# Attention and a mixture of experts on one core: order constants refitted, later rows of the second batch, one more unit in blocks

## The chip, the cores and the metric

The kernel runs on one core of a Trainium2 chip. The metric is the device time of one execution in microseconds; the time of a kernel is the median of its runs. TensorE (PE) does the matmuls, with its weight loads shown apart as PEld; VectorE (DVE) and ScalarE (ACT) take results out of the accumulation banks and form sums; GpSimd (POOL) and SyncE (SP) mostly issue DMAs.

## What is computed

Four batches of windowed attention with four sink columns, whose output feeds a mixture of four experts. Every expert works on every token; its result is weighted by a normalised probability.

```python
# q, k, v: 4 batches, 8 heads, 768 rows, 64 columns; n_sink 4, window 128
keep = is_sink | in_window                 # columns 0..3, and the last 128 up to the row
scores = where(keep, q @ k.T / sqrt(64), -1e9)
a = exp(scores - max(scores)); a = a / (sum(a) + 1e-9)
x = (a @ v) laid out as 3072 tokens x 512
# x: 3072 x 512; w1: 4 x 512 x 1024; w2: 4 x 1024 x 512
p = domain_probs / (sum(domain_probs) + 1e-9)
for e in range(4):
    out += p[:, e:e+1] * (relu(x @ w1[e]) @ w2[e])
```

All matmuls take bf16 operands.

## The kernel before

**Tiles and stages.** Each batch `b` has three groups `g` of 256 tokens, and each group four head pairs. Attention on a group has a score step for each pair (L679, into banks named `sps`), exponentials on ScalarE (L704), a mask on VectorE (L698, or L713 in batch 0), the value step (L738 and L745, banks `od`), reciprocals (L772) and a scaling (L784 on ScalarE). The normalised rows are turned into `xT`, by TensorE in batch 0 (L803) and by a DMA from SP after that (L762).

**Rows of q and k.** They come by POOL's DMA queue in tiles of 128 rows (`load_nat`, L229, into `qkn`). In batch 0 TensorE turns them (L573). From batch 1 on, `turn_nat` (L241) turns a tile with a transposing DMA from SP into `qkT`. There is one `qkT` buffer, so a batch's tiles can be turned only after the last scores of the batch before it. The first scores of a batch need its first two tiles, group 1 two more, and from batch 2 on one set of sink scores (L640) needs all six. V comes by `load_v` (L294) into six tiles `vx`, each free after the values of the batch before.

**The experts.** A unit is one (batch, group, expert). A plain unit does `x @ w1` in 32 matmuls of 256 columns (L1053, banks `hps`). A unit in blocks ("fast", `emit_fast`) does the same as a 2 x 2 block product in Winograd's form: seven products P1 to P7 of 8 matmuls of 128 columns (L1140, banks `cps`), with sums between them on VectorE (L1193, L1208) and copies on ScalarE (L1186, L1199). It needs sums of the weights (`weight_form1`, L372 to L378, four for an expert, the last in place of a quarter of w1) and of the tokens (L1109). `START` says from which (batch, group) on an expert's units are in blocks. The second layer is plain in batch 0 (L1392, 512 columns) and in the block form in the others (L1314, 256 columns), with sums of w2 from `weight_form` (L336 to L342) and of the activations (L1237, L1258).

**The order.** The program is written out instruction by instruction by a planner in the kernel itself. It keeps a clock for each engine (`t["pe"]` and so on), and in each turn picks the next piece for TensorE: a step of attention, a part of a unit, a product of the second layer. Each comes with the time at which the planner thinks it is ready and a rank; the lowest rank among the ready ones wins. Work of VectorE and ScalarE is put into a list with a ready time and a slack (`later`), and `flush` emits, in order of due time, what fits. All engines run their instructions in the order that comes out, and wait for one another by semaphores; so the planner's constants set the order and nothing else. `turned_at` is the planner's time for a turned tile, `next_form` queues the next weight sum on VectorE (w1 first), and `ahead` is the batch whose attention is being interleaved (0 during the first).

```python
if ahead:
    next_form()
if ahead + 1 < B and not att.more() and ... mix.done >= sum(work[:ahead]) * LEAD[ahead - 1]):
    ahead += 1
    att = Attention(ahead)
...
opts = [(max(r, now), (DUE if due else 3) - 0.1 * (step == "two"), "att", step) for r, step in att.options()]
```

Of the kernel before, what the change touches and what calls it, by code (L numbers as in the profile page):

```python
# [16 lines left out]
def kernel(  # L17
# [17 lines left out]
    E, Dm, F = moe_w1.shape  # L35
# [22 lines left out]
    ]  # L58

    NGATE = 5  # L60
    START = {0: (1, 0), 1: (0, 2), 2: (0, 0), 3: (2, 1)}
    MIX = 3
    SHARE_OF = (0.98, 0.90, 1.01)
    LEAD = (0.91, 0.90)
    DUE = 1.5
    LOW_PRODUCT = 2.005
    LOW_SECOND = 2.7
    HIGH_PRODUCT = 1.9
    EARLY = 0.01
    MASK = 2500  # L70
    GATE = 1500
    GATE0 = 500
    FORM = 9000
    TOKEN = 1000
    MARGIN = 2000
    HOLD = 0
    FULL = 7
    STEP0 = 0.3
    READY = 40
    WIDE = 2  # L80
    OPEN = 2.6
    ONACT = 1
    ONE = 2
    PAIR = 1
# [3 lines left out]
    BIASED = 1  # L88
    FAST = tuple(START)
    BZ = 0  # L90
# [9 lines left out]
    FLIP, LATE, SLOW = 300, 2500, 1500  # L100
# [78 lines left out]
    landed = {}  # L179
# [12 lines left out]
    def sp(*deps, issue=530, takes=600, turning=False):  # L192
        t["sp"] = max([t["sp"], *deps]) + issue
        at = max(t["hw"], t["sp"] + 800)
        row = next((x[3] for x in moved if x[1] <= at < x[2]), 0.0)
        if turning and row:
            t["hw"] = at + TURNED * (row + SHARE)
            t["sw"] += TURNED * SHARE
            for x in moved:
                if x[2] > at:  # L200
                    x[1] += TURNED * SHARE * (x[1] > at)
                    x[2] += TURNED * SHARE
                    landed[x[0]] = x[2] + 900
                    if x[0][0] == "w1" and ("w1", x[0][1]) in landed:
                        landed["w1", x[0][1]] = max(landed["w1", x[0][1]], x[2] + 900)
        else:
            t["hw"] = at + takes + max(0.0, min(takes, t["sw"] - at)) * (not turning)
        return t["hw"] + 900
# [15 lines left out]
    qkn_free, scored_at = [0.0] * NQB, {}  # L224
# [12 lines left out]
    def turn_nat(b, tb):  # L237

        if b not in qkT:
            qkT[b] = sb.tile([P, 2, NHP, S], BF16, name="qkT", tag="qkT", bufs=1)  # L240
        nc.sync.dma_start(  # L241
            out=qkT[b][:, :, :, tb * P:(tb + 1) * P].rearrange("c i h p -> c (i h) p"),
            in_=nat[b, tb].rearrange("p i h d -> p (i h d)"), transpose=True,
        )
        turned_at[b, tb] = sp(landed["qk", b, tb], scored_at.get(b - 1, 0.0), issue=1330, takes=1400, turning=True) + LATE
        qkn_free.remove(1e12)
        qkn_free.append(turned_at[b, tb])
        qkn_free.sort()
# [106 lines left out]
    spared_at = {}  # L355
    forms1, formed1, forms1_at, left1 = {}, {}, {}, [NG * START[e][0] + START[e][1] for e in range(E)]

# [33 lines left out]
    def form_due(e):  # L391
        n = formed.get(e, 0)
        if e == E - 1 and spared_at.get("w2", 1e12) > t["pe"]:
            return False
        return landed.get(("w2", e), 1e12) + 9000 < t["pe"] and (n < 3 or n == 3 and e in used)
# [3 lines left out]
    def next_form():  # L399

        if forming:
            return False
        x = next(((weight_form1, e) for e in FAST if form1_due(e)), None) or next(
            ((weight_form, e) for e in range(E) if form_due(e)), None)
        if x is None:
            return False

        def run(engine):
            forming.clear()
            x[0](x[1])  # L410
        forming.append(x)
        later("dve", t["pe"], FORM, run)
        return True
# [143 lines left out]
    turned_at, sinkA_at, aT_at, onat_at, xT_at = {}, {}, {}, {}, {}  # L557
# [362 lines left out]
    class Mixture:  # L920
# [25 lines left out]
        def is_fast(self, b, g, e):  # L946
            return (b, g) >= START[e]

# [49 lines left out]
        def firsts(self):  # L998
# [12 lines left out]
            if n < WIDE and early:  # L1011
                at, g = self.next_early()
                yield at, (OPEN if n else 2), ("early", g)
            if n < WIDE and self.units and early <= MIX and self.room() and not (early + zero and self.live >= NH - 1):
                yield self.unit_ready(*self.units[0], False), (OPEN if n else 2) - EARLY, ("unit",)

# [68 lines left out]
        def tokens(self):  # L1085
# [22 lines left out]
            def run(engine):  # L1108
# [4 lines left out]
                else:  # L1113
                    self.T_at[b, g] = done
            later("dve", at, TOKEN, run)

        def emit_fast(self, u, m, ready):
# [64 lines left out]
            if m == "P1":  # L1182
                u["last"] = join(2, lambda at: gated(H[:, 1, :, 1], tiles["X"], 1, at, GATE, slots["X"]))

# [19 lines left out]
            elif m == "P2":  # L1204
                gated(H[:, 0, :, 1], y, 1, end, GATE, slots["Y"])
            elif m == "P7":
# [5 lines left out]
            elif m == "P3":  # L1212
                gated(H[:, 0, :, 0], y, 0, end, GATE, slots["V"])
            else:
# [212 lines left out]
    ahead, upto, loaded, wide = 0, 0.0, 0, 0  # L1427
# [22 lines left out]
    while mix.more() or att.more():  # L1450
        now = t["pe"]

        if not att.more() and ahead == B - 1 and not wide:
            wide = 1
            mix.widened()
        if not att.more() and not loaded:
            loaded = 1
            gates_by_row()
            turns += [(1, tb) for tb in range(NQB)]
            loads.append((load_w1, 3))  # L1460
            for tb in range(NQB):
                loads.append((load_nat, 1, tb))
                if tb % 2:
                    loads += [(load_v, 1, (tb - 1,)), (load_v, 1, (tb,))]
            loads.append((load_w2, 3))
        x = next((x for x in loads if load_ready(x) < now + 1500), None)
        if x and t["pool"] < now + 1500 and free_ring(x):
            loads.remove(x)
            x[0](*x[1:])
        if turns and (ahead < 2 or not mix.second) and landed.get(("qk", *turns[0]), 1e12) < now and (turns[0][0] <= ahead or turns[0][0] == ahead + 1 and not att.todo):  # L1470
            x = turns.pop(0)
            turn_nat(*x)
            b = x[0]
            if b in (1, B - 1) and x[1] == NQB - 1:
                spare_rows("w2" if b == 1 else "w1")
            if 0 < b < B - 1 and x[1] == NQB - 1:
                nc.gpsimd.tensor_copy(out=held, in_=qkT[b][:, 1, NHP - 1, S - 2:S])
                pool(2, turned_at[x])
                nat_loads(b + 1, range(NQB))
                turns += [(b + 1, tb) for tb in range(NQB)]  # L1480
        flush(now)
        mix.tokens()
        mix.chore()
        if ahead:
            next_form()
        if ahead + 1 < B and not att.more() and (ahead == 0 or (ahead + 1, 0) in turned_at) and (ahead == 0 or mix.done >= sum(work[:ahead]) * LEAD[ahead - 1]):
            ahead += 1
            att = Attention(ahead)
            upto = mix.done
        share = (sum(work[:ahead]) - upto) * SHARE_OF[max(ahead - 1, 0)]  # L1490
        due = ahead == 0 or att.steps * share <= (mix.done - upto) * att.total
        opts = []
        if att.more():
            opts = [(max(r, now), (DUE if due else 3) - 0.1 * (step == "two"), "att", step) for r, step in att.options()]
        s2, p = mix.second_ready(), mix.product_ready()
        behind = max(t["dve"] - now, 0.0) + 500 * sum(x[2] == "dve" and x[0] < now + 300 for x in pend)
        opts.append((max(p, now), HIGH_PRODUCT if behind > BEHIND or mix.live >= FULL else LOW_PRODUCT, "product", None))
        opts += [(max(f, now), p, "first", x) for f, p, x in mix.firsts()]
        opts.append((max(s2, now), 1 if mix.since >= 1 else LOW_SECOND, "second", None))
        soonest = min(o[0] for o in opts)  # L1500
        if soonest > now + 40 and flush(soonest, True):
            continue
        if soonest < 20000 and soonest > now + 220:
            idle_products(acc[1], 1, G)
            continue
        if soonest > 1e11:
            if loads:
                x = loads.pop(0)
                x[0](*x[1:])
            else:  # L1510
                turn_nat(*turns.pop(0))
            continue
        r, _, kind, step = min(opts, key=lambda o: (o[0] > now + 40, o[0] if o[0] > now + 40 else 0, o[1]))
        assert r < 1e11
        if kind == "att":
            att.emit(step)
        elif kind == "first":
            mix.emit_first(step, r)
        elif kind == "product":
            mix.emit_product()  # L1520
        else:
            mix.emit_second()
# [36 lines left out]
```

## Time and profile before

| | |
|---|---|
| median of 3 runs | 364.03 us (363.68 to 364.74) |
| the profiled execution | 364.39 us |
| its span, first to last instruction | 362.7 us |
| granted TensorE clock | 1.000 |
| matmuls, weight loads | 4400, 4412 (rows in the trace) |
| idle time of ScalarE before L1186 | 44.0 us, for TensorE |
| idle time of POOL before L1477 | 31.5 us, for turning copies |

The profile is of one execution. A group line gives the source line, the engine, the operation, output and inputs, and how many there were; "idle" is the time in which the engine stood still just before, with what ended it. An engine's idle time matters only if TensorE in the end waits for it. In the timeline the first two columns are the start and the length in us, and a bracket gives the wait just before. The shown length of a matmul is longer than the distance to the next one, since matmuls overlap; distances between starts tell the rate.

```profile
q0 software_dynamic: 77520, 17.31, 55.0%
q1 hardware_dynamic: 38668, 18.75, 25.5%
```

These are the two large DMA queues, with packets, MB and the share of the time of 16 DMA engines: q0 is POOL's (loads), q1 holds SP's.

### The profile page before, as it was taken

What the parts mean: (1) busy time and instruction counts of PE and PEld (TensorE: products, weight loads), DVE (VectorE), ACT (ScalarE), POOL (GpSimd) and SP (SyncE); (2) the same over time, 40 slices, a digit from 0 to 9 for tenths busy, and PEclk for the clock granted to TensorE, in tenths of its full rate; (3) what the DMA queues carried; (4) which work ended last, traced back from release to release, by engine and by line L of the source; (5) the groups of instructions that cost most, each with busy time, mean ns of one, the idle gap of its engine ahead of it and who ended that gap; (6) DMA issues with size and microseconds to landing.
All of it is one profiled execution on the core that took longest, in us unless ns stands there. A gap on an engine that the chain in (4) does not pass through costs nothing.

```text
span 362.7 us, 10537 instructions
## 1 busy us (share of the span) xinstructions
PE 354.3 (98%) x4400; PEld 298.7 (82%) x4412; DVE 298.7 (82%) x669; ACT 164.1 (45%) x417; POOL 71.5 (20%) x92
## 2 busy tenths in 40 slices
PE   8899999899999999999999999999999999999996
PEld 4585767666768878899899899999999999999985
DVE  6854998976598979869989979979999799897850
ACT  5864733569554683842554455455213222313210
POOL 8935116500816151150200000000000000000000
DMA  9999999999999989499871211322012012100011
GB/s 167 166 184 195 210 212 158 127 169 206 150 171 136 151 118 149 55 186 146 124 95 33 58 60 34 42 74 62 17 38 74 24 44 60 31 31 31 2 61 58
DMA packets 117291, 37.25 MB, mean 103 GB/s; under 512 B 100612, under 2 KB 112740, under 8 KB 117244
## 3 DMA queue, kind: packets, MB, share of 16 engines
q0 software_dynamic: 77520, 17.31, 55.0%
q1 hardware_dynamic: 38668, 18.75, 25.5%
q8 instruction: 34, 0.56, 0.6%
q10 hardware_dynamic: 1056, 0.52, 0.5%
q14 instruction: 13, 0.11, 0.1%
HBM read 40.45 MB, written 6.34 MB: 129 GB/s over the span
## 4 chain that ended last, share of the span: by engine, by line
PE 78%; DMA 16%; POOL 2%; DVE 1%; ACT 1%; issue 1%; SPq 0%
PE acc L1314 31%; PE cps L1140 29%; PE hps L1053 7%; DMA w<-in_moe_w_dram 7%; DMA qkn<-in_k_dram 6%; PE acc L1392 5%; DMA qkT<-qkn 3%; PE sps L679 2%; PE od L745 2%; POOL qkn L229 1%; PE od L738 1%; POOL vx L294 1%; ACT aT L704 1%; POOL sel L482 0%; PE sinks L640 0%
## 5 line engine op out<-in xcount | busy, mean ns | idle before, releaser
L1140 PEld LDWEIGHTS <-w 128*128 128x128 bf16 x1152 | 71.8, 98 | 4.4 <-issue 1.5
L1314 PEld LDWEIGHTS <-H 128*128 128x128 bf16 x600 | 55.8, 98 | 6.1 <-issue 0.6
L704 ACT ACTIVATE aT<-sps 128x512 bf16<-128x512 f32 (+1 forms) x96 | 47.1, 577 | 16.2 <-PE sps L679 16.0
L1173 DVE SCALAR_TENSOR_TENSOR H<-cps,gates 128x512 bf16<-128x512 f32 x78 | 52.8, 683 | 0.8
L1140 PEld LDWEIGHTS <-vf 128*128 128x128 bf16 x744 | 45.9, 98 | 2.3 <-issue 0.8
L1314 PE MATMUL acc<-w,H 128*128 128x256 bf16 x360 | 47.7, 273 | 0.0
L1053 PE MATMUL hps<-xT,w 128*128 128x256 bf16 x384 | 47.3, 273 | 0.0
L1392 PE MATMUL acc<-w,H 128*128 128x512 bf16 x180 | 43.6, 379 | 0.9 <-issue 0.5
L1140 PE MATMUL cps<-T,w 128*128 128x128 bf16 x576 | 43.9, 219 | 0.5 <-DVE cps L1193 0.5
L784 ACT ACTIVATE onat<-od,R 128x64 bf16<-128x64 f32 x144 | 33.4, 331 | 24.0 <-DVE R L772 23.9
L1140 PE MATMUL cps<-xT,w 128*128 128x128 bf16 x576 | 43.4, 219 | 0.0
L1186 ACT COPY cps<-cps 128x512 f32<-128x512 f32 x36 | 20.7, 575 | 47.8 <-PE cps L1140 44.0
L1053 PEld LDWEIGHTS <-w 128*128 128x128 bf16 x384 | 36.1, 98 | 5.9 <-issue 0.8
L1140 PE MATMUL cps<-T,vf 128*128 128x128 bf16 x496 | 37.5, 219 | 0.0
L1392 PEld LDWEIGHTS <-H 128*128 128x128 bf16 x192 | 18.0, 98 | 18.1 <-issue 0.3
L294 POOL DMA_DIRECT2D vx<-in_v_dram x24 | 21.6, 913 | 42.0 <-PE od L745 30.1
L1314 PEld LDWEIGHTS <-S 128*128 128x128 bf16 x288 | 27.0, 98 | 3.1 <-issue 0.4
L1193 DVE TENSOR_TENSOR cps<-H,cps 128x512 f32<-128x512 f32 x30 | 20.7, 691 | 9.3 <-PE cps L1140 9.3
L698 DVE TENSOR_TENSOR aT<-aT,mask 128x1024 bf16<-128x1024 bf16 (+1 forms) x36 | 22.8, 639 | 5.7 <-ACT aT L704 5.7
L1364 ACT COPY osb<-acc 128x256 f32<-128x256 f32 x28 | 10.5, 383 | 35.6 <-PE acc L1314 35.6
L1208 DVE TENSOR_TENSOR H<-H,cps 128x512 f32<-128x512 f32 x30 | 20.5, 682 | 4.2 <-PE cps L1140 4.0
L1066 ACT ACTIVATE H<-hps 128x512 bf16<-128x512 f32 x27 | 16.1, 597 | 16.2 <-PE hps L1053 15.8
(128 smaller groups left out, 561.0 us busy)
## 6 DMA issues: line engine op xcount, KB each, us to landing
w<-in_moe_w_dram POOLq DMA_DIRECT2D x7, 1024.0 KB, 16.7
out_dram<-osb SPq DMA_DIRECT2D x19, 256.0 KB
gates<-gate_rows SPq DMA_DIRECT2D x36, 128.0 KB
vx<-in_v_dram POOLq DMA_DIRECT2D x24, 128.0 KB, 6.9
qkn<-in_q_dram POOLq DMA_DIRECT2D x22, 128.0 KB, 6.7
qkn<-in_k_dram POOLq DMA_DIRECT2D x22, 128.0 KB, 6.8
w<-in_moe_w_dram POOLq DMA_DIRECT2D x2, 512.0 KB, 8.8
out_dram<-aT SPq DMA_DIRECT2D x4, 256.0 KB
```

Of the source, the lines that this page charges most:

```text
L294: nc.gpsimd.dma_start(out=vx[tb][:, :, 0:D], in_=v[b, :, tb * P:(tb + 1) * P, :].rearrange("h p d -> p h d"),)
L698: nc.vector.tensor_mul(a, a, m[:, None, :].to_broadcast([P, 2, w]))
L704: nc.scalar.activation(out=a[:, ph], in_=sps[ph][:, 0:w], func=AF.Exp, scale=scale)
L784: nc.scalar.mul(o[:, qi, hp, ph * D:(ph + 1) * D], od[:, qi, ph, 0:D], R[:, qi, ph])
L1053: nc.tensor.matmul(h[:, i].rearrange("p (q n) -> p q n", q=2), lhsT=w1_sb[e][:, db, fb * P:(fb + 1) * P], rhs=xT[b, g][:, :, db], start=(i ...
L1140: nc.tensor.matmul(y[:, f], lhsT=A[:, d, f * P:(f + 1) * P], rhs=T[:, d], start=(m in ("P1", "P5") and f == 0 and d == 0), stop=(d == 1), ...
L1173: nc.vector.scalar_tensor_tensor(out=dst, in0=src, scalar=0.0, in1=gate, op0=ALU.max, op1=ALU.mult)
L1186: nc.scalar.copy(out=tiles["Y"], in_=y)
L1193: nc.vector.tensor_add(tiles["V"], c5, tiles["X"])
L1208: nc.vector.tensor_add(c5, c5, y)
L1314: nc.tensor.matmul(x, lhsT=self.operand(b, g, e, m)[:, f], rhs=forms[e][m][:, f], start=(k == 0 and f == 0 and m in (("P1", "P5", "P2") if ...
L1392: nc.tensor.matmul(op, lhsT=H[:, fb // QF, fb % QF, s], rhs=w2_sb[e][:, fb, :], start=(fb == 0), stop=(fb == NFB - 1),)
```

## The change

Only constants of the planner change, and three conditions:

- `START[0]` goes from (1, 0) to (0, 2): the unit of batch 0, group 2, expert 0 is done in blocks.
- The planner counts a turned tile of batch 1 as ready 1500 ns later (`ROWS1`); the copy itself is the same.
- `next_form` may be called from planner time 21000 ns on (`SOON`), also while the first batch's attention runs; in that time it takes sums of w1 only, since sums of w2 now need `ahead`.
- The ranks and slacks of the planner: attention that is due has rank 0 instead of 1.5 (`DUE`), a product has rank 1 instead of 1.9 when VectorE is behind (`HIGH_PRODUCT`), units of batch 1 may start while four units of batch 0 are left instead of three (`MIX`), attention of batches 2 and 3 starts later (`LEAD`), and the due times of gated evictions (`GATE`), token sums (`TOKEN`) and second-layer sums (`MARGIN`) move.

```diff
-    START = {0: (1, 0), 1: (0, 2), 2: (0, 0), 3: (2, 1)}
-    MIX = 3
+    START = {0: (0, 2), 1: (0, 2), 2: (0, 0), 3: (2, 1)}
+    MIX = 4
     SHARE_OF = (0.98, 0.90, 1.01)
-    LEAD = (0.91, 0.90)
-    DUE = 1.5
+    LEAD = (0.92, 0.94)
+    DUE = 0
...
-    HIGH_PRODUCT = 1.9
+    HIGH_PRODUCT = 1
...
-    GATE = 1500
+    GATE = 3000
...
-    TOKEN = 1000
-    MARGIN = 2000
+    TOKEN = 5000
+    MARGIN = 1000
...
+    SOON = 21000
+    ROWS1 = 1500
...
-        turned_at[b, tb] = sp(landed["qk", b, tb], ..., turning=True) + LATE
+        turned_at[b, tb] = sp(landed["qk", b, tb], ..., turning=True) + LATE + ROWS1 * (b == 1)
...
-            ((weight_form, e) for e in range(E) if form_due(e)), None)
+            ((weight_form, e) for e in range(E) if ahead and form_due(e)), None)
...
-        if ahead:
+        if ahead or now > SOON:
             next_form()
```

The two lines added among the constants move every later line number up by two; the text keeps the numbers of the kernel before.

More of the change, by code (lines that the diff above doesn't have):

```diff
@@ L244, in turn_nat @@
         )
-        turned_at[b, tb] = sp(landed["qk", b, tb], scored_at.get(b - 1, 0.0), issue=1330, takes=1400, turning=True) + LATE
+        turned_at[b, tb] = sp(landed["qk", b, tb], scored_at.get(b - 1, 0.0), issue=1330, takes=1400, turning=True) + LATE + ROWS1 * (b == 1)
         qkn_free.remove(1e12)
```

## The prediction

> **What bounds the kernel now.** I read the page's busy shares first, then its chain and its slices.
>
> ```profile
> PE 354.3 (98%) x4400; PEld 298.7 (82%) x4412; DVE 298.7 (82%) x669; ACT 164.1 (45%) x417; POOL 71.5 (20%) x92
> ...
> DVE  6854998976598979869989979979999799897850
> ...
> PE 78%; DMA 16%; POOL 2%; DVE 1%; ACT 1%; issue 1%; SPq 0%
> ```
>
> TensorE is busy almost throughout, and the chain runs through it for 78% of the span. The 16% of DMA all lies before 72 us, where TensorE has other work while rows and weights land. Busy does not mean dense, so next I asked for the merged chain in order of time, where long pieces give the price of one matmul.
>
> ```profile
> 137.53 3.49 PE hps L1053 x32
> ...
> 160.60 2.68 PE cps L1140 x48
> ```
>
> A 256-column matmul costs 3.49 / 32 = 109 ns and a 128-column one 2.68 / 48 = 56 ns. From 40 us on, nearly all starts of neighbouring matmuls keep these distances, so the end moves only with the matmul work, with the price of changing to scores and back, and with the few real waits. For those I read the waits of TensorE and the timeline around them.
>
> ```profile
> PE sps L679 <- DMA qkT<-qkn: 0.9, 1, 0.9
> PE cps L1140 <- DVE cps L1193: 0.5, 1, 0.5
> ```
>
> ```profile
> 70.37 0.61 PE L1140 MATMUL cps<-T,w 128*128 128x128 bf16 x8
> 71.89 0.34 PE L679 MATMUL sps<-qkT 64*128 64x256 bf16 x4 [0.91 <-DMA qkT<-qkn]
> 72.16 0.62 PE L1140 MATMUL cps<-T,vf 128*128 128x128 bf16 x8
> 72.62 1.89 PE L1392 MATMUL acc<-w,H 128*128 128x512 bf16 x7
> 74.35 0.35 PE L745 MATMUL od<-vx,aT 128*128 128x65 bf16 x6
> 74.63 0.34 PE L679 MATMUL sps<-qkT 64*128 64x256 bf16 x4
> 74.90 0.28 PE L1140 MATMUL cps<-T,vf 128*128 128x128 bf16 x2
> ```
>
> The first scores of the second batch could have begun at 70.8 (8 matmuls of 56 ns after 70.37, and the change) and begin at 71.89: the turned rows are 1.07 us late by start times. The same rows price a change. Six value matmuls of 29 ns end at 74.52 and the scores start at 74.63; four score rows run two at a time, 384 columns in 0.16, and the next line starts 0.27 after them. So each run of scores costs 0.11 + 0.11, about 0.2 us, beyond its columns. Two other waits are worth naming.
>
> ```profile
> 83.85 0.87 PE L679 MATMUL sps<-qkT 64*128 64x128 bf16 x12
> 84.81 0.22 PE L738 MATMUL od<-vsd,sinkA 128*128 128x130 bf16 x1
> ...
> 102.69 0.62 PE L679 MATMUL sps<-qkT 64*128 64x128 bf16 x12
> 103.24 1.05 PE L1053 MATMUL hps<-xT,w 128*128 128x256 bf16 x8
> ...
> 123.29 0.87 ACT L704 ACTIVATE aT<-sps 128x384 bf16<-128x384 f32 x2 [0.57 <-PE sps L679]
> 123.78 0.61 PE L1140 MATMUL cps<-T,w 128*128 128x128 bf16 x8 [0.53 <-DVE cps L1193]
> ```
>
> Twelve score rows take 0.55 to the next line at 102.69 but 0.96 at 83.85: 0.41 lost there, in waits for the exponentials that free score banks. At 123.04 the last score row is followed by L1140 only 0.74 later instead of 0.14: 0.60 lost to a VectorE sum. Before 40 us there are further gaps, but TensorE's order is the same in both kernels up to about 42 us.
>
> **The change, part by part.** The counts are of the instructions in the two built programs.
>
> *One more unit in blocks (batch 0, group 2, expert 0).* It removes 32 matmuls of L1053 (32 x 109 = 3.49 us) and adds 7 products of 8 matmuls of L1140 (56 x 56 = 3.12): -0.37. Its token sums exist already, for expert 1. VectorE gets three instructions more and ScalarE two, of about 0.6 us each; they lie beside TensorE, and any one without cover costs its 0.6. The weight loads go from 32 to 56, 98 ns each, and stay hidden: the 48 matmuls above have one each and run at 56 ns.
> The Trainium skill (Perfetto Trace Analysis, Identifying the Most-Contended Engine) holds the busy share of weight loads, not that of matmuls, for the measure of how close TensorE is to its limit. Counted so, the 24 loads more would cost 2.35 us and this part would come out at about +2; the 56 ns row does not agree.
>
> *Order refitted.* Scores now stand in 32 unbroken runs instead of 34: 2 x 0.2 = -0.4. The last products, from the last unit to the last store, are the same in number and order: 0.
>
> *Rows counted as ready later.* Ahead of the first score row of the second batch now stand 80 more matmuls of L1140 and 32 fewer of L1053: 4.48 - 3.49 = +0.99 us of TensorE work. The q and k loads and the turning copies stand in the same order on POOL and SP up to there, and their issue is held by earlier landings, so they land as before. TensorE arrives at 70.77 + 0.99 = 71.76 against 71.8: at most 0.1 of the 1.07 stays, -0.97. Bounds: -1.07 if the rows come a little earlier, 0 if they come 1 us later.
>
> *Sums of w1 queued in the first batch.* The four sums for expert 0 (L372 to L378, 0.60 us each back to back) move from about 45 to 57 us to about 25 to 30 us, where the slices show VectorE at 4 to 5 tenths instead of 8 to 9. The w1 of expert 0 landed at 21.4, expert 1 at 36.5 (its first sum now comes near 41): no wait on DMA. Cost 0; uncovered, each delays one handoff by 0.6.
>
> *Handoffs in the new order.* I took every wait of TensorE on VectorE or ScalarE, and compared TensorE's rows between producer and consumer with the rows along the other engine's queue. In the old order this finds shortages of 0.39 and 0.56 us where the trace lost 0.41 and 0.60. In the new order these two are gone. The worst new one is at the first values of batch 2: 0.2 from the scores to ScalarE, 0.87 for two exponentials, 0.56 for the mask make 1.65 with the hop, against 1.5 us of TensorE work (8 matmuls of L1053, one run of 8 score rows, two changes), and an eviction of L1066 may stand ahead: 0.4 short. Five more places are short by 0.03 to 0.11, 0.36 in all. So 1.01 becomes 0.77: -0.24. Bounds: -1.0 (all covered) and +0.6 (one more 0.6 us row in the way).
>
> *SP and POOL.* Batch 2's turning copies now stand behind four output stores instead of two, the last of which gets its data 0.3 us after the scores that free the rows' buffer; with an issue of up to 1.4 that delays them under 2 us, and from those scores to the first that need the rows lie 14.7 us of TensorE work, where 4.6 are needed. On POOL, three value loads of batch 2 pass ahead of the last six q/k loads, 3 x 0.88 = 2.6 us. Those scores of batch 1 end near 110.7 instead of 103.2, so the last of the six lands near 121.8 + 7.5 + 2.6 = 131.9 and is turned 3.6 later, at 135.5; it is needed near 138.4, 5.4 later than before: 0, with 3 us to spare. Batch 3's copies are tighter, and are a rival below.
>
> Sum: -0.37 - 0.4 - 0.97 - 0.24 = -1.98. The span of 362.70 becomes 360.7; 1.69 us lie around it (364.39 - 362.70), so the profiled execution would take 362.4. That execution was 0.36 above the median of the runs, 364.03. From the median the sum gives 362.05. Part of the 0.36 may be the late rows themselves, so I take 362.2, between the two.
>
> **The rivals.**
> *The rows are late again.* For: in the trace fifteen of the sixteen parts of the second tile had counted by 69.90 and the last only at 71.75, a straggler that can fall elsewhere, and 0.1 us is no margin. Against: even the fifteen parts were early by 1.9. If it lands 1 us later, the wait is back: 362.2 + 1.0 = 363.2.
> The Trainium skill (DMA: Bandwidth & Descriptors, Why a DMA increments its semaphore by 16 and not by 1) says that the sixteen engines finish independently and only the full count means landed; the trace agrees, by the two times above.
>
> *Batch 3's rows take over, and the kernel is slower.* Its rows can only be turned after batch 2's last scores. Between those and batch 3's first scores stood 27.3 us of TensorE work; now 8.8 (44 matmuls of L1314, 24 of L1053, 8 of L1140, values and changes). Two turning copies need, from the first issue to the second's landing, 7.2 us at this place in the trace (151.6 to 158.8), 4.6 for batch 2 (103.4 to 108.0), but 13.2 for batch 1 (58.6 to 71.8), among weight loads. At 13.2, with 0.2 to issue, the wait is 4.6: 366.8. It makes the kernel slower from about 10.6 us on. Against: the q/k loads that fill the DMA engines there in the trace wait, in the new order, for these very copies to land, and one value load alone comes between.
>
> *VectorE becomes the bound.* For: 9 tenths in most slices. Against: a 512-element row occupies it 0.60, not the 0.68 shown, as back-to-back starts tell. Four w1 sums in the wrong place: 4 x 0.6 = 2.4, 364.6.
>
> *Weight loads bound.* 24 x 98 ns instead of the 0.37 saved: 362.2 + 0.37 + 2.35 = 364.9.
>
> **How the numbers follow.** The forecast gets 0.68 (own range 361.4 to 363.2: all handoffs covered, or one row more), late rows 0.17, batch 3's rows 0.09, VectorE 0.04, weight loads 0.02. About 0.3%, 1.1 us, is what a measurement of this kernel can tell from no change, so faster means under 362.94. Forecast, with a little of it lost above that line, and a third of the late rows make 0.71 faster; batch 3's rows and a little of VectorE make 0.10 slower; 0.19 remain. The range, 361.2 to 364.2, takes in the forecast and the late rows, and leaves out the last three and some ends.
>
> **What would show it.** Right: the first score row of batch 2 (the second one) starts near 71.8 without a wait over 0.2; 32 runs of scores; L1140 has 56 rows more and L1053 32 fewer at the same 56 and 109 ns; the first values of batch 2 wait about 0.4; the last matmul lies some 2 us earlier. Wrong: a wait on turned rows over 0.5 us at any batch, or new VectorE waits of more than 0.8 in sum.

## The result, and the profile after

| | before | after |
|---|---|---|
| first pair: median (lowest to highest of 6 runs) | 364.15 us (363.34 to 365.11) | 362.32 us (362.24 to 362.44) |
| the profiled execution, and its span | 364.39, 362.7 | 362.36, 360.7 |
| the same pair again, in a later group of runs: median (middle half of the runs) | 364.49 (364.04 to 364.94) | 362.44 (362.02 to 362.84) |

The ratio is 0.9933, with a 95% interval of 0.991 to 0.9957; in the repeat it is 0.9941 (0.9924 to 0.9959). The ratios leave out runs more than 1.5% above the fastest of the same kernel, which takes out six runs, all of them of kernels with a moved DMA. Line numbers after are higher by two: L1142 is the old L1140, L1055 the old L1053, L681 the old L679.

The page of the changed kernel, its busy shares, its VectorE slices and the engines of its chain:

```profile
PE 354.0 (98%) x4436; PEld 297.8 (83%) x4436; DVE 299.2 (83%) x671; ACT 165.6 (46%) x419; POOL 71.3 (20%) x92
...
DVE  6775989896588989789879989969999898897850
...
PE 88%; DVE 6%; ACT 2%; DMA 1%; issue 1%; POOL 1%; ACTq 0%; DVEq 0%
```

The shares of busy time say nothing: TensorE stands at 98% in both. (Twelve matmuls of L1392 have no record in the trace of the kernel before, so the real rise in matmuls is 24 and not 36.) The chain tells the change. Its DMA part falls from 16% to 1%, because the chain no longer runs back through the turned rows at 72 us into the loads; it now stays on TensorE. The slices for 18 to 36 us (the third and fourth digits) rise from 5 and 4 to 7 and 5: those are the sums of w1, moved there.

The groups by line and shape (busy time, mean ns of one, idle time before them), first of the kernel before and then of the changed one, and the pieces of the merged chain after, first for the 256-column and then for the 128-column matmul:

```profile
L1140 PE MATMUL cps<-T,w 128*128 128x128 bf16 x576 | 43.9, 219 | 0.5 <-DVE cps L1193 0.5
L1140 PE MATMUL cps<-xT,w 128*128 128x128 bf16 x576 | 43.4, 219 | 0.0
L1053 PE MATMUL hps<-xT,w 128*128 128x256 bf16 x384 | 47.3, 273 | 0.0
L1140 PE MATMUL cps<-T,vf 128*128 128x128 bf16 x496 | 37.5, 219 | 0.0
```

```profile
L1142 PE MATMUL cps<-T,w 128*128 128x128 bf16 x592 | 45.0, 219 | 0.1
L1142 PE MATMUL cps<-xT,w 128*128 128x128 bf16 x592 | 44.7, 219 | 0.0
L1055 PE MATMUL hps<-xT,w 128*128 128x256 bf16 x352 | 43.6, 273 | 0.0
L1142 PE MATMUL cps<-T,vf 128*128 128x128 bf16 x512 | 37.4, 219 | 0.0
```

```profile
41.70 1.75 PE hps L1055 x16
...
115.77 2.69 PE cps L1142 x48
```

32 plain matmuls are gone and 16 + 16 + 16 more in blocks are seen here (8 others are in a smaller group). The rates are the old ones, 1.75 / 16 = 109 ns and 2.69 / 48 = 56 ns. Next TensorE's waits, as what it waited for, the sum in us, how often and the longest; and its timeline where the old kernel waited for turned rows:

```profile
PE acc L554 <- DVE lent L465: 1.4, 1, 1.4
PE sps L681 <- DVE xT L267: 0.4, 1, 0.4
PE tx L805 <- DVE onat L777: 0.3, 2, 0.2
PE od L747 <- DMA vx<-in_v_dram: 0.3, 1, 0.3
PE od L747 <- DVE aT L700: 0.3, 1, 0.3
```

```profile
70.97 0.61 PE L1142 MATMUL cps<-T,vf 128*128 128x128 bf16 x8
71.42 0.61 PE L1142 MATMUL cps<-xT,w 128*128 128x128 bf16 x8
71.97 0.34 PE L681 MATMUL sps<-qkT 64*128 64x256 bf16 x4
72.24 1.90 PE L1394 MATMUL acc<-w,H 128*128 128x512 bf16 x8
```

The scores of batch 1 start at 71.97, which is 8 matmuls of 56 ns and one change behind 71.42: no wait. In this execution the sixteen parts of the second tile had all landed by 71.25. The wait on DVE aT is the handoff that the prediction put at the first values of batch 2:

```profile
125.17 0.87 ACT L706 ACTIVATE aT<-sps 128x384 bf16<-128x384 f32 x2
125.92 0.51 PE L681 MATMUL sps<-qkT 64*128 64x256 bf16 x8
126.07 0.56 DVE L700 TENSOR_TENSOR aT<-aT,mask 128x768 bf16<-128x768 bf16 x1
...
126.69 0.35 PE L747 MATMUL od<-vx,aT 128*128 128x65 bf16 x6 [0.26 <-DVE aT L700]
```

The exponentials end at 126.04, the mask at 126.63, the values start at 126.69; eight score rows after 125.92 would have let them start 0.33 earlier.

**Where the time came from.** I compared the starts of TensorE's rows from 41 us to the last matmul: 317.96 us before, 315.85 after, 2.11 less. A run of scores that nothing disturbs costs 0.20 us beyond its columns in both traces. The wait for the rows accounts for 0.98 of the 2.11. Two old handoffs (0.41 at 83.85 and 0.59 at 123.04) are gone and two new ones (0.33 at 126.22, 0.11 at 124.69) have come: 0.56. Behind 41 us there are 22 runs of scores instead of 24: 0.41. The unit: 0.37. That is 2.32; 0.2 went back. In part it went to the two runs of 18 score rows behind sink scores, at 82.26 and 98.86: with the sinks each costs 0.57 beyond its score columns, where the old run of 6 behind sinks, at 97.23, costs 0.44.

### The profile page after: what moved, and what is told of

It is laid out like the page before. It is cut to its first block, busy times and chain, and to the rows that moved or that the text cites. A ratio compares the mean times of both kernels' runs of the same rounds, so it can differ in the third digit from the quotient of the medians.

```text
span 360.7 us, 10596 instructions
## 1 busy us (share of the span) xinstructions
PE 354.0 (98%) x4436; PEld 297.8 (83%) x4436; DVE 299.2 (83%) x671; ACT 165.6 (46%) x419; POOL 71.3 (20%) x92
## 4 chain that ended last, share of the span: by engine, by line
PE 88%; DVE 6%; ACT 2%; DMA 1%; issue 1%; POOL 1%; ACTq 0%; DVEq 0%
PE cps L1142 31%; PE acc L1316 29%; PE acc L1394 11%; PE hps L1055 10%; PE od L747 3%; PE sps L681 3%; DVE H L1175 2%; DMA vx<-in_v_dram 1%; ACT aT L706 1%; PE od L740 1%; DVE S L1260 1%; PE tx L805 1%; DVE onat L777 1%; DVE H L1210 1%; DVE osb L1404 0%
## 5 line engine op out<-in xcount | busy, mean ns | idle before, releaser
L1142 PEld LDWEIGHTS <-w 128*128 128x128 bf16 x1184 | 73.6, 98 | 4.2 <-issue 1.3
L1142 PEld LDWEIGHTS <-vf 128*128 128x128 bf16 x768 | 47.0, 98 | 1.9 <-issue 0.3
L1394 PE MATMUL acc<-w,H 128*128 128x512 bf16 x192 | 45.3, 379 | 0.0
L1142 PE MATMUL cps<-T,w 128*128 128x128 bf16 x592 | 45.0, 219 | 0.1
L1142 PE MATMUL cps<-xT,w 128*128 128x128 bf16 x592 | 44.7, 219 | 0.0
L1055 PE MATMUL hps<-xT,w 128*128 128x256 bf16 x352 | 43.6, 273 | 0.0
L1142 PE MATMUL cps<-T,vf 128*128 128x128 bf16 x512 | 37.4, 219 | 0.0
L1055 PEld LDWEIGHTS <-w 128*128 128x128 bf16 x352 | 33.0, 98 | 4.5 <-issue 0.6
L1316 PE MATMUL acc<-wf,H 128*128 128x256 bf16 x176 | 23.8, 273 | 0.0
```

What stands on the lines that cost most here:

```text
L1055: nc.tensor.matmul(h[:, i].rearrange("p (q n) -> p q n", q=2), lhsT=w1_sb[e][:, db, fb * P:(fb + 1) * P], rhs=xT[b, g][:, :, db], start=(i ...
L1142: nc.tensor.matmul(y[:, f], lhsT=A[:, d, f * P:(f + 1) * P], rhs=T[:, d], start=(m in ("P1", "P5") and f == 0 and d == 0), stop=(d == 1), ...
L1316: nc.tensor.matmul(x, lhsT=self.operand(b, g, e, m)[:, f], rhs=forms[e][m][:, f], start=(k == 0 and f == 0 and m in (("P1", "P5", "P2") if ...
L1394: nc.tensor.matmul(op, lhsT=H[:, fb // QF, fb % QF, s], rhs=w2_sb[e][:, fb, :], start=(fb == 0), stop=(fb == NFB - 1),)
```

## The experiments

Each group of runs has its own runs of the kernel before beside it: 364.61 median beside the two padded kernels and the two runs that take a part out of the change, 364.49 beside the repeat and the three parts alone, 364.55 beside the three with a moved DMA, 364.33 beside the last. "Middle half" is the range from the first to the third quartile.

**Is the old time, and its spread, a wait for a landing?** Idle matmuls in front of the first scores of batch 1 tell: where TensorE waits there, they cost nothing.

```diff
         c = 0
+        if b == 1 and b not in scored_at:
+            for i in range(19):
+                nc.tensor.matmul(sps[0][:, 0:P], lhsT=ident, rhs=ident, start=True, stop=True)
```

In the kernel before:

> The kernel before with 19 idle matmuls of 128 columns (19 x 56 ns = 1.06 us of TensorE work, results overwritten) right ahead of the first scores of batch 1, nothing else moved. Theory (the first scores wait for a landing that varies from run to run; without a wait the old order takes 364.39 - 1.07 = 363.32): the padding takes the place of the wait, so the median rises only from about 364.15 to between 364.4 and 364.7, the fastest run lies near 364.4 instead of 363.3, the spread of the runs shrinks from 1.8 us to under 0.9, and the profile shows a wait of under 0.3 us on turned rows. Rival (the wait on the landing is not what the old time and its spread consist of): the padding is paid in full, median 365.2, spread as before.

In the changed kernel:

> The changed kernel with the same 19 idle matmuls at the same place. Theory (TensorE arrives at 71.97 after rows that landed at 71.25, so nothing there waits for a landing): paid in full, 362.32 + 1.06 = 363.4, spread still about 0.2 us. Rival (in the changed kernel the landing still sets the first scores, and the trace only happened to show no wait): less than 0.6 us is added.

The padded old kernel took 364.46 (364.00 to 365.10, middle half 364.17 to 364.78) against 364.61 (363.41 to 367.74, middle half 364.05 to 365.14); ratio 0.999 (0.9975 to 1.0004). The padded new kernel took 363.34 (middle half 363.30 to 363.44). The timeline of the padded old kernel:

```profile
70.59 1.22 PE L677 MATMUL sps<-ident 128*128 128x128 bf16 x19
71.75 0.34 PE L682 MATMUL sps<-qkT 64*128 64x256 bf16 x4
```

In the old kernel 1.06 us of added work costs nothing that can be measured and the scores still start at 71.75, without a wait: the padding stands where the wait stood. In the new one the same work is paid in full, 363.34 - 362.32 = 1.02. The spread shrank in the old kernel as expected, though to 1.1 us and not under 0.9. Not all of the old spread is this wait: the two slowest runs of the kernel before in this group, 367.05 and 367.74, had a mean granted clock of 0.995, and no trace of such a run was kept. Without the wait the two kernels thus take about 364.46 - 1.06 = 363.40 and 363.34 - 1.06 = 362.28; a little waiting may be left in the first, since in three of the eleven traces compared below the rows land later than 71.75. The 2.05 between the kernels in the repeat are 1.12 of TensorE's order and some 0.9 of waiting.

**Is nothing left of that wait?** The changed kernel once more:

> The changed kernel once more, on the chip and beside the kernel before of this group, for a like-for-like pair. Theory (no wait on a landing is left on TensorE's path): 362.3, with the middle half of the runs within 0.2 us, where the kernel before has 1.1. Rival (the small spread of the first six runs was luck, landings still reach the path): a middle half as wide as that of the kernel before.

362.44 median, 361.94 to 363.41, middle half 0.8 us wide. The rival is right: landings still reach the path. Whether the narrow spread of the first six runs was luck or belonged to their chip is not shown; none of the six is as fast as the five fastest here (361.94 to 362.05). The timeline of this profiled execution (362.85):

```profile
71.53 0.61 PE L1142 MATMUL cps<-xT,w 128*128 128x128 bf16 x8
72.44 0.34 PE L681 MATMUL sps<-qkT 64*128 64x256 bf16 x4 [0.30 <-DMA qkT<-qkn]
```

The second tile's last part landed at 72.39 here, 0.57 behind the fifteenth, and TensorE, there at 72.08, waited. Over the eleven traces in which POOL issues its loads in the old order the last part comes between 69.64 and 72.39. TensorE arrives at 70.9 before the change, ahead of most of these, and at 72.0 after it, behind most. The chain of this execution holds 17% of DMA again: a wait of 0.30 us is enough to lead it back through the rows, so that share tells where the chain runs and not how much was lost.

**The parts of the change, one at a time.** The early sums taken out of the changed kernel (`SOON = 1e12`):

> The changed kernel with the sums of w1 queued only from the second batch on, as before (SOON beyond the end). The planner then makes 34 runs of scores instead of 32, with all matmuls the same in number. Theory (a run of scores costs 0.2 us; a handoff short by the distance of the rows costs just that): +0.2 for the runs... in sum 0.19 of TensorE work, and handoffs short by 0.64 (ahead of a plain unit before batch 1's scores) and 0.41 instead of 0.11, 0.11 and 0.41: +0.4. Together 362.32 + 0.6 = 362.9. Rival (the early sums are worth nothing, my costing at 0 taken alone): 362.3 to 362.5. Rival (VectorE is near its bound, and 2.4 us of sums come back): 364.7.

The later rows taken out of it (`ROWS1 = 0`):

> The changed kernel with the turned rows of batch 1 counted as ready at their own time again (ROWS1 0). The planner's order then brings the first scores of batch 1 1.33 us of TensorE work earlier, has 33 runs of scores, and 0.67 us more TensorE work and changes in all. Theory: TensorE arrives at 71.97 - 1.33 = 70.64 while rows land at 71.2 to 71.8, so a wait of 0.6 to 1.2 us is back, and so is a spread of the runs of over 0.8 us; handoffs short by 0.97 near batch 2's first scores and 0.4 near 141 us add about 1.5: 362.32 + 0.67 + 0.9 + 1.5 = 365.4. Rival (the constant only shifts rows, and the handoffs are hidden): 362.3 + 0.9 = 363.2.

363.13 and 365.41, where 362.9 and 365.4 were forecast from counts of rows. Without the early sums the two waits that the count named are there:

```profile
72.38 0.34 PE L681 MATMUL sps<-qkT 64*128 64x256 bf16 x4 [0.26 <-DMA qkT<-qkn]
...
78.47 0.62 PE L1142 MATMUL cps<-T,w 128*128 128x128 bf16 x8
79.61 1.03 PE L1055 MATMUL hps<-xT,w 128*128 128x256 bf16 x8 [0.52 <-ACT onat L786]
```

The first is the landing again (72.34 in that trace); the second is the scaling whose place on ScalarE depends on VectorE's row order: 8 matmuls of 56 ns after 78.47 it could have begun at 78.92, so 0.69 is lost by start times, where 0.64 was counted. Without the later rows the wait on the rows is back, and the handoffs near batch 2's first scores lose 1.2 by start times, where 0.97 was counted (the waits of that kernel):

```profile
PE sps L681 <- DMA qkT<-qkn: 1.0, 1, 1.0
PE tx L805 <- DVE onat L777: 0.5, 3, 0.2
PE cps L1142 <- DVE cps L1195: 0.5, 1, 0.5
PE sps L681 <- DVE xT L267: 0.4, 1, 0.4
PE od L747 <- DVE H L1175: 0.4, 1, 0.4
PE od L740 <- ACT onat L786: 0.4, 1, 0.4
```

One part alone in the kernel before: the unit (`START[0]` to (0, 2)), the later rows (`ROWS1`), the ranks and slacks.

> The kernel before with the unit (batch 0, group 2, expert 0) in blocks and nothing else changed. Theory (TensorE's work falls by 0.22 in the order that the old ranks then give; the first scores of batch 1 come 0.37 earlier in that work, so the wait on the rows grows by as much; handoffs are short by 0.73 near 115 to 120 us, 0.32 near 74, 0.21 and 0.12, against 0.39 and 0.56 before): +0.4 to +0.6 on the kernel before. Rival (the unit is worth its 0.37 by itself): -0.4.

> The kernel before with the turned rows of batch 1 counted as ready 1500 ns later and nothing else changed. The planner then puts 2.62 us more of TensorE work ahead of batch 1's first scores, and makes 36 runs of scores instead of 34. Theory (no wait on the rows: -0.9; 0.57 us more of TensorE work and changes; handoffs short by up to 1.11 near 128 us and 0.49 near 144 instead of 0.95: +0.65): +0.3 on the kernel before, with a middle half of the runs under 0.4 us. Rival (taking that wait away is worth its size in any order): -1.0.

> The kernel before with the refitted ranks, slacks and start points alone (MIX, LEAD, DUE, HIGH_PRODUCT, GATE, TOKEN, MARGIN as in the changed kernel; old START, no later rows, no early sums). Theory (0.42 us more of TensorE work, 35 runs of scores; the first scores of batch 1 at the same work as before, so the same wait and the same spread; handoffs short by 0.39, 0.97 and 1.02 instead of 0.39 and 0.56: +1.4): +1.8 on the kernel before, 366.2. Rival (the refit of the order is a gain by itself, 0.64 by my sum): -0.6.

| alone in the kernel before | median | ratio to before (95%) |
|---|---|---|
| unit in blocks | 364.90 | 1.0012 (0.9992 to 1.0031) |
| later rows | 363.63 | 0.9974 (0.9955 to 0.9994) |
| ranks and slacks | 366.84 | 1.007 (1.0049 to 1.0092) |

The unit alone gains nothing that can be measured (+0.4 to +0.6 was forecast, +0.41 measured), and the ranks alone cost 2.35, where 1.8 was forecast. Its waits have about the sizes that were counted: by start times 0.2 near 84, 1.2 at 124 to 128 and 1.1 at 150 to 151, against 0.39, 0.97 and 1.02 (the timeline of the kernel with the ranks alone):

```profile
71.69 0.34 PE L679 MATMUL sps<-qkT 64*128 64x256 bf16 x4 [0.99 <-DMA qkT<-qkn]
...
124.25 0.34 PE L745 MATMUL od<-vx,aT 128*128 128x65 bf16 x6 [0.44 <-DVE H L1173]
128.17 0.61 PE L1140 MATMUL cps<-T,w 128*128 128x128 bf16 x8 [0.50 <-DVE cps L1193]
150.69 0.22 PE L738 MATMUL od<-vsd,sinkA 128*128 128x130 bf16 x1 [0.43 <-ACT onat L784]
151.51 0.22 PE L738 MATMUL od<-vsd,sinkA 128*128 128x130 bf16 x1 [0.30 <-ACT onat L784]
```

The later rows alone are a miss of mine: +0.3 expected, -0.86 measured. The wait went, and the middle half of the runs shrank to 363.58 to 363.84, as it should where TensorE reaches the scores at 73.2. But of the 1.6 that I counted for short handoffs, 1.11 near 128 and 0.49 near 144, the trace shows 0.9 by start times, 0.45 at 127 and 0.46 at 135, and nothing near 144:

```profile
126.65 0.34 PE L746 MATMUL od<-vx,aT 128*128 128x65 bf16 x6
127.28 0.61 PE L1141 MATMUL cps<-xT,w 128*128 128x128 bf16 x8 [0.28 <-ACT onat L785]
...
135.58 0.60 PE L1054 MATMUL hps<-xT,w 128*128 128x256 bf16 x4 [0.39 <-DVE H L1174]
```

The count treats each shortage of a group as if nothing before it had held TensorE back. I read the difference so that the loss of 0.45 at 127 gave VectorE the time that the places behind it were short of; that was not tried by itself. Alone, the three add to 364.5 + 0.4 - 0.9 + 2.35 = 366.4; together, and with the early sums, they make 362.4. What a constant of the planner is worth depends on the order that it meets.

**Earlier rows instead of a later TensorE.** W1 of expert 3 lands at 56.5 and is first read near 78, ahead of the rows in POOL's queue. One DMA is moved behind them, and every other instruction of every engine keeps its place:

```diff
+            def start(i=i):
+                nc.gpsimd.dma_start(out=w1_sb[e]..., in_=moe_w1[e]...)
+            if e == E - 1:
+                waiting.append(start)
+            else:
+                start()
```

`waiting` is run behind the loads of `load_nat(1, 1)`. In the kernel before, in the changed kernel, and in the changed kernel with one more unit in blocks:

> The kernel before with one DMA moved on POOL: the w1 of expert 3 (first read near 78 us, landed at 56.5) is issued behind the four q and k loads of batch 1's first two tiles instead of ahead of them. Every other instruction keeps its place. Theory (the old time and its spread hold a wait for the landing of those tiles): the tiles' loads land some 5 us earlier, by about 55, and the second turning copy near 66 instead of 71.5 to 72.5; the wait at 71 us is gone: 363.4 (from the padded kernel: 364.46 - 1.06), 1.1 under the kernel before, with the middle half of the runs inside 0.4 us. Rival (the wait is hidden by something that is late behind it, or w1 of expert 3 becomes late): 364.5, or more.

> The changed kernel with the same one DMA moved, every other instruction in its place. Theory (at 71.97 TensorE still meets a late landing in about half of the runs, 0.36 us in the second profile of the changed kernel): the time falls from 362.44 to the fastest run of the changed kernel, 361.9 to 362.0, with the middle half of the runs inside 0.2 us. Rival (the spread of the changed kernel has another source): 362.4, spread as it was. Taken with the run above: what is left between the two kernels without the wait, 1.4, is the worth of the unit (0.37), of the runs of scores (0.41) and of the handoffs (0.56).

> The kernel of the run above with one further unit in blocks (batch 2, group 0, expert 3; START[3] is (2, 0)) and three slacks set so that the runs of scores stay 32 and stand where they stood (STEP0 0.5, MARGIN 0, MASK 2000). Theory (a unit in blocks is worth 32 x 109 - 56 x 56 ns where the order around it stays, and its three VectorE and two ScalarE rows are covered): -0.37, less 0.08 for handoffs newly short by 0.09 and 0.1: about 361.6 to 361.7. Rival (VectorE, at 9 tenths there, has no room, each row costs its 0.6): +1.4, 363.4. Rival (24 more weight loads count in full): +2.4, 364.3.

All three missed: 367.01 (363.48 to 369.81), 364.83 (363.52 to 369.53) and 366.76 (362.81 to 370.48), with ratios to the kernel before of 1.0039 (1.0005 to 1.0073), 1.0017 (0.9988 to 1.0046) and 1.0022 (0.9986 to 1.0057). The rows did what was foreseen; the last part of the second tile landed at 66.27, 65.83 and 67.53, and the wait there was gone; so the third run says nothing on the unit. The time was lost 18 us later (timeline of the changed kernel with the moved DMA):

```profile
71.88 0.34 PE L689 MATMUL sps<-qkT 64*128 64x256 bf16 x4
...
89.07 0.61 PE L1150 MATMUL cps<-T,vf 128*128 128x128 bf16 x8
91.36 1.89 PE L1402 MATMUL acc<-w,H 128*128 128x512 bf16 x8 [1.68 <-DMA w<-in_moe_w_dram]
```

That is w2 of expert 3, the last of the weight loads. In the changed kernel its sixteen parts land from 87.18 to 87.83 and it is first read at 89.61. Here the first part lands earlier, at 86.62, but the last two at 91.09 and 91.32, 4 us behind the other fourteen. In the old kernel with the moved DMA one part falls back, to 93.60; in the third run two do, to 90.40 and 92.52. I had named w1 of expert 3 as what might become late, and not asked how much the last weight load had to spare: 1.8 us. Why these parts fall back so far was not tried.

The wait is not the whole loss. The timeline of the old kernel with the moved DMA, and behind it one stretch of TensorE there (from and to, length, busy time, granted clock, share and rate of DMA):

```profile
93.64 3.33 PE L1400 MATMUL acc<-w,H 128*128 128x512 bf16 x8 [2.04 <-DMA w<-in_moe_w_dram]
...
93.92:97.33 3.41, 3.41 (x14) 0.50 1.14 145
```

From just after this wait of 2.04 us, and likewise around the end of the one of 2.89 us in the third run, the granted clock of TensorE stands at 0.50 for 3.41 us, which costs about 1.7 us more (3.41 x 0.50). Eight matmuls of 512 columns take 3.33 us in it, against 1.89 behind the wait of 1.68, where the clock stayed at 1.00. Of the 36 runs of the three kernels, the 18 with a mean granted clock of 0.995 or less all took 366.6 or more; the other 18 took 366.7 or less. So a good part of the spread is the clock after the wait, and not the wait itself.

**A later TensorE without the padding, and one more unit.** What the runs point to is real work in front of the scores, and no DMA moved:

```diff
-    START = {..., 3: (2, 1)}
+    START = {..., 3: (2, 0)}
...
-    MASK = 2500
+    MASK = 2000
...
-    MARGIN = 1000
+    MARGIN = 0
...
-    nat = {}
+    nat, held_off = {}, [1, 2]
...
+        if held_off and 1 not in scored_at and ahead == 1:
+            rest = [o for o in opts if o[2] != "att"]
+            if min(opts, key=...)[2] == "att":
+                opts = rest
+                held_off.pop()
```

> The changed kernel with no DMA moved. The planner passes over the first scores of batch 1 twice, so that 2.17 us of TensorE work (8 matmuls of L1392 and 8 of L1140, which stood behind those scores) goes ahead of them; MASK 2000 brings the order back to the old one from about 82 us on. And the one further unit in blocks of the run before (START[3] (2, 0), MARGIN 0). 32 runs of scores, as in the changed kernel. Theory (what is left in the changed kernel is the wait for the rows in some runs, and a unit in blocks is worth 0.37 where the order stays): TensorE reaches the first scores near 74.1, past every landing seen so far (at most 72.4), and w2 of expert 3 is first read at the same time as before, 0.8 to 1.6 after its landing; 361.94 (the fastest run of the changed kernel, without the wait) - 0.43 of TensorE work = 361.5, with the middle half of the runs inside 0.3 us. Rival (the padded kernel's small spread came from the idle matmuls, and real work ahead of the scores makes the exponentials or the fourth tile, with 1.7 us to spare, late): 362.4 or more. Rival (VectorE has no room for the unit's rows): 363 or more.

362.05 median (361.86 to 362.11, middle half 362.00 to 362.10), ratio 0.9925 (0.9897 to 0.9953). The timeline:

```profile
73.51 0.61 PE L1142 MATMUL cps<-T,w 128*128 128x128 bf16 x8
74.05 0.50 PE L681 MATMUL sps<-qkT 64*128 64x256 bf16 x8
...
191.55 1.06 PE L1142 MATMUL cps<-xT,w 128*128 128x128 bf16 x16
192.72 0.34 PE L747 MATMUL od<-vx,aT 128*128 128x65 bf16 x6
```

The scores start at 74.05, the rows landed at 72.04, and all runs lie within 0.25 us: the wait is gone. The size missed by 0.55. I had taken the fastest run of the changed kernel, 361.94, for its time without the wait; the padded run, on another chip, gives 362.28. From there the kernel gained 0.23 instead of 0.43. The values at 192.72 now wait: 16 matmuls of 56 ns after 191.55 they could have begun at 192.44, so 0.28 is lost by start times, where the count of rows said 0.09. In the changed kernel the second 8 of these 16 were 8 matmuls of L1055, which cover 0.4 us more. The unit and the later arrival were not run apart. The interval of this kernel overlaps that of the changed kernel, so it is the fastest here by its median, by 0.3 to 0.4, but not by the ratio.

## Why the prediction was right, step by step

The time of 362.2 and its sum, -1.98, held: the profiled execution was predicted at 362.4 and took 362.36. That the two agree to 0.04 us is partly luck: the handoffs gave 0.32 more than forecast, and 0.2 in longer runs of scores and small losses, and 0.1 ahead of 41 us, went back. The signs named for it came too: the first scores start at 71.97, there are 32 runs of scores, and the last matmul starts at 357.27 instead of 359.30. Point by point:

- *The unit, -0.37.* Counts and rates are as told (+56 and -32 rows, 56 and 109 ns). The 24 further weight loads cost nothing that the rows show; after another 24, in the last kernel, the matmuls of L1142 still run at 56 ns. So the rule that the prediction cited (the Trainium skill, Perfetto Trace Analysis, Identifying the Most-Contended Engine) does not set the time here. But alone, in the old order, the unit gains nothing. The 0.37 is worked out from counts and rates; no run took the unit alone out of the changed kernel.
- *Runs of scores, -0.4.* Measured 0.20 for each and two fewer: -0.41. The Trainium skill (TensorEngine Tiling (Array Packing), Key Properties) says that changing the tiling mode drains TensorE, and gives no time; the scores, on 64 rows, are such a change, and 0.20 is its price here, in and out. Not foreseen: where 18 score rows stand in one run behind sink scores, 0.13 comes back.
- *Later rows, -0.97.* The mechanism is shown by the padding and by `ROWS1 = 0`. The size was right for the profiled pair (0.98), by two slips that cancel: the 70.8 in the prediction leaves the change out (70.37 + 0.45 + 0.11 = 70.93), so the old wait was 0.96 to 0.98 and not 1.07, and none of it stayed. Over many runs the old wait is about 364.5 - 363.4 = 1.1, and about 0.16 of it is still in the changed kernel (362.44 - 362.28, if the chips of these two groups are alike): the margin of "at most 0.1" was as thin as the rival said.
- *Sums of w1, 0.* Mis-sized. Without them the changed kernel takes 0.7 more (363.13 against 362.44), with two runs of scores more. The sum had put what they bring under the handoffs, which were counted in the finished order.
- *Handoffs, -0.24.* Measured -0.56. The worst one was named at its place, 0.4 short, and lost 0.33. Of the five lesser ones, 0.36 in all, one of 0.11 showed: the sum of new losses was 0.44 and not 0.77.
- *SP and POOL, 0.* Right, the time itself by luck. The last of the six tiles for the sinks of batch 2 was turned at 135.46 (predicted 135.5) and is first read at 137.5. But its loads had landed by 129.69 instead of 131.9, and SP issued its turning copy only at 131.64, behind two gate copies and an output store.

The rivals. *Rows late again* happened in the repeat: 0.30 waited in the profiled run, and runs up to 363.41. *Batch 3's rows* did not take over: with 8.8 us of work between the batches the two copies took 4.7 us (first issue 168.94, second landing 173.60), like those of batch 2, and the first scores started at 177.45. *VectorE* and *weight loads* as bounds fell with the runs above. The wait on `vx` at 9.6 us was not foreseen; it is made up before 38.3, where this trace is 0.09 behind the old one.

## What to carry to other kernels

Where one engine is busy 98% of the time, count its rows between each producer and its consumer. Here the few short distances, the fixed price of each change of kind and the wait on a landing made up what the order won, and they did not add up constant by constant. Runs that spread wider than those of a padded kernel were here a sign of a wait on a landing, and idle work put in front of the wait measured it. Before a load is moved ahead, look at what the last load of its queue has to spare.

## What the runs showed that was not expected

- The landing of the second tile's turning copy varied by 2.75 us (69.64 to 72.39, issued at 59.60 to 61.84, in eleven traces of ten kernels), by 1.14 between two executions of the changed kernel (71.25 and 72.39), and its last part of sixteen trailed the fifteenth by 0.0 to 1.85 us.
- With the one DMA moved, the last part of a 1 MB load landed 4.7 us after its first (86.62 to 91.32), against 0.65 in the changed kernel (87.18 to 87.83), and the runs spread over 6 us or more.
- Behind waits of TensorE of 2.04 and 2.89 us its granted clock stood at 0.50 for 3.41 us; behind one of 1.68 us it stayed at 1.00.
